# Linear attention and a four-expert block in one kernel: the attention of the next chunk put between the expert matmuls of this one

## The chip, the cores and the metric

One core of a Trainium2 chip. The metric is the device time of one execution in microseconds (us), taken over several runs; the profile is one execution, whose span is some 2 to 3 us shorter than the time. Engines: TensorE (PE for matmuls, PEld for its weight loads), VectorE (DVE), ScalarE (ACT), GpSimd (POOL); SP issues the transfers of the sync queue.

## The reference, cut to what matters

```python
# attention: B, H, S, D = 4, 8, 768, 48; f = sigmoid(f_logit)
for t in range(S):
    state = f[:, :, t, :, None] * state + einsum('bhd,bhe->bhde', k[:, :, t], v[:, :, t])
    y[:, :, t] = einsum('bhd,bhde->bhe', q[:, :, t], state)
x = y.transpose(0, 2, 1, 3).reshape(B * S, H * D)          # 3072 x 384
# four experts, F = 1024, every row goes through all of them
p = domain_probs / (domain_probs.sum(-1, keepdims=True) + 1e-09)
for e in range(4):
    out += p[:, e:e+1] * (maximum(x @ w1[e], 0) @ w2[e])
```

Both kernels cut time into 6 chunks of 128 steps. Within a chunk the attention is a masked score matmul plus a matmul with the state carried from the chunk before, so chunks of one batch follow each other. The four batches are independent.

## The kernel before

Attention first, one batch and one chunk at a time, x written to DRAM; then the experts over groups of 512 rows. The order inside each engine is chosen by a scheduler.

```python
for b in range(B):
    for c in range(C):
        # four loads of 128 x 384 f32 (q, k, v, f): runs of 192 bytes
        nc.scalar.activation(out=sig, in_=fg, func=AF.Sigmoid)
        nc.scalar.activation(out=gneg, in_=sig, func=AF.Ln)
        nc.tensor.matmul(out=cs, lhsT=Ub, rhs=gneg, ...)          # cumulative sum, 384 columns
        nc.scalar.activation(out=ecsQ, in_=cs, func=AF.Exp)
        nc.vector.reciprocal(out=ecsK, in_=ecsQ)
        # Qp = qg * ecsQ, Kp = kg * ecsK, vgb = vg, all on POOL
        # gs: 8 column sums; egs = exp(gs)
        # 16 transposes of 128 x 48 into tp, two copies to Qt, Kt
        for h in range(H):                                        # scores
            nc.tensor.matmul(out=AT_ps[:, ...], lhsT=Kt[:, ...], rhs=Qt[:, ...], ...)
        # AT = AT_ps * mask
        for h in range(H):                                        # y: 48 rows, then 128 rows
            nc.tensor.matmul(out=y_ps[:, hs], lhsT=Qt[:, ts], rhs=state_bf[:, hs], ...)
            nc.tensor.matmul(out=y_ps[:, hs], lhsT=AT[:, ts], rhs=vgb[:, hs], ...)
        # store y; KV; state = (state + KV) * egs, 8 multiplies of 48 x 48 on POOL
# ...
nc.gpsimd.dma_start(out=w1_sb, ...)       # cast f32 -> bf16, 3 MB each; no wait, so it starts early
nc.gpsimd.dma_start(out=w2_sb, ...)
for g in range(6):
    # load x, 12 transposes, then per expert e:
    for fc in range(8):
        for kk in range(3): nc.tensor.matmul(out=h_ps, ...)        # 512 columns
        nc.vector.tensor_relu(out=h_sb[:, fc, :], in_=h_ps)
    for nt in range(4):
        for fc in range(8): nc.tensor.matmul(out=o2_ps, ...)       # 384 columns
        # o_sb += p * o2_ps on DVE
```

## Time and profile before

| | us |
|---|---|
| time, median of 3 runs | 565.63 |
| span of the profiled run | 562.4 |
| attention, from the first matmul on | about 289 |
| experts | about 264 |

How the busy shares, the slices, the chain of waits and the two stretches are read is told in the prediction, with the lines.

### The profile page before, as it was taken

To read this page: it belongs to the slowest core of one execution; us is meant where nothing else is said; L and a number is where in the kernel's file an instruction comes from. 1 tells how busy PE (TensorE), PEld (TensorE's weight loads), DVE (VectorE), ACT (ScalarE), POOL (GpSimd) and SP (SyncE) were. 2 spreads that over 40 slices of the span, in tenths; PEclk is the share of its full clock that TensorE was granted. 3 is DMA by queue.
4 is the path that set the end of the run, shared out by engine and by line. 5 is a ranking of instruction groups with operands and counts; after the bars stand their busy time and mean duration, and the time that the engine had idled before them with its cause. 6 is when DMAs were issued, how large, how long until landed. Compare 5 with 4: busy or idle time off the path is not lost.

```text
span 562.4 us, 7147 instructions
## 1 busy us (share of the span) xinstructions
PE 421.2 (75%) x2760; PEld 253.2 (45%) x2784; DVE 319.7 (57%) x420; ACT 164.4 (29%) x285; POOL 139.3 (25%) x290
## 2 busy tenths in 40 slices
PE   0044158566556556566879999999999999999996
PEld 0033036445445445445654555545555555544443
DVE  1056244554554454464436776777777777677674
ACT  5096374574664674551111000000000000000000
POOL 4142364535536535635720000000000000000000
PEclk9999999999999999999999999999999999999999
DMA  9989834444443343231001101001001001001001
GB/s 165 197 143 187 158 68 94 107 92 85 103 94 80 76 94 64 63 77 41 24 23 28 30 0 58 23 7 58 1 29 58 0 1 57 2 1 56 1 0 57
DMA packets 118498, 35.12 MB, mean 62 GB/s; under 512 B 103616, under 2 KB 116928, under 8 KB 118464
## 3 DMA queue, kind: packets, MB, share of 16 engines
q1 hardware_dynamic: 112800, 28.37, 23.8%
q0 software_dynamic: 5664, 6.29, 6.7%
q8 instruction: 22, 0.36, 0.3%
q14 instruction: 12, 0.10, 0.1%
HBM read 33.87 MB, written 7.08 MB: 73 GB/s over the span
## 4 chain that ended last, share of the span: by engine, by line
PE 57%; POOL 11%; DVE 10%; issue 9%; DMA 4%; ACT 2%; SPq 0%; POOLq 0%; ACTq 0%; DVEq 0%
PE o_ps L199 23%; PE h_ps L193 22%; POOL state L145 8%; PE y_ps L130 4%; DVE ecsK L91 4%; DVE AT L120 3%; PE y_ps L128 3%; PE tp L112 3%; POOL Kp L98 3%; DVE Kt L113 2%; DMA fg<-in_f_logit_dram 2%; DMA kg<-in_k_dram 2%; PE xT_ps L182 1%; POOL Qp L97 1%; DVE h_sb L195 1%
## 5 line engine op out<-in xcount | busy, mean ns | idle before, releaser
L195 DVE TENSOR_SCALAR h_sb<-h_ps 128x512 bf16<-128x512 f32 x192 | 129.3, 692 | 26.5 <-PE h_ps L193 22.7
L199 PE MATMUL o_ps<-w_sb,h_sb 128*128 128x384 bf16 x768 | 142.9, 326 | 0.0
L193 PE MATMUL h_ps<-xT,w_sb 128*128 128x512 bf16 x552 | 139.0, 380 | 2.1 <-issue 0.2
L199 PEld LDWEIGHTS <-h_sb 128*128 128x128 bf16 x768 | 71.5, 98 | 65.2 <-DVE h_sb L195 13.6
L91 DVE RECIPROCAL ecsK<-ecsQ 128x384 f32<-128x384 f32 x24 | 61.2, 2552 | 65.7 <-POOL Kp L98 46.2
L193 PEld LDWEIGHTS <-w_sb 128*128 128x128 bf16 x576 | 56.4, 98 | 59.4 <-issue 3.4
L145 POOL TENSOR_SCALAR state<-state,egs 48x48 f32<-48x48 f32 x192 | 72.4, 398 | 3.4 <-DVE state L142 2.4
L185 ACT COPY xT<-xT_ps 128x128 bf16<-128x128 bf16 x72 | 14.3, 275 | 186.4 <-PE xT_ps L182 126.5
L205 DVE SCALAR_TENSOR_TENSOR o_sb<-o_ps,pt,o_sb 128x384 f32<-128x384 f32 x72 | 44.5, 618 | 38.3 <-PE o_ps L199 38.3
L130 PE MATMUL y_ps<-vgb,AT 128*128 128x48 bf16 x192 | 42.8, 223 | 29.9 <-DVE AT L120 29.9
L87 PE MATMUL cs<-gneg,Ub 128*128 128x384 bf16 x24 | 11.5, 480 | 63.8 <-ACT gneg L84 59.1
L130 PEld LDWEIGHTS <-AT 128*128 128x128 bf16 x192 | 20.2, 105 | 75.5 <-DVE AT L120 65.3
L113 DVE COPY Kt<-tp 48x1024 bf16<-48x1024 bf16 x24 | 16.4, 683 | 58.3 <-PE tp L112 58.3
L174 POOL TENSOR_TENSOR pt<-pt,psum 128x16 f32<-128x16 f32 x6 | 1.2, 214 | 190.1 <-DVE psum L173 190.1
L128 PE MATMUL y_ps<-state_bf,Qt 48*128 48x48 bf16 x192 | 42.3, 220 | 3.4 <-ACT state_bf L123 3.4
L102 PEld LDWEIGHTS <-gneg 128*48 128x48 bf16 x192 | 12.0, 131 | 58.2 <-issue 57.8
L94 POOL CAST vgb<-vg 128x384 bf16<-128x384 f32 x24 | 12.1, 504 | 103.7 <-PE y_ps L130 92.4
L117 PE MATMUL AT_ps<-Qt,Kt 48*128 48x128 bf16 x192 | 24.8, 308 | 8.2 <-DVE Kt L113 8.1
L123 ACT CAST state_bf<-state 48x384 bf16<-48x384 f32 x24 | 12.3, 511 | 63.7 <-POOL state L145 54.5
L120 DVE TENSOR_TENSOR AT<-AT_ps,mask 128x1024 bf16<-128x1024 f32 x24 | 28.2, 1174 | 3.3 <-PE AT_ps L117 3.3
L97 POOL TENSOR_TENSOR Qp<-qg,ecsQ 128x384 bf16<-128x384 f32 x24 | 23.7, 990 | 24.8 <-ACT egs L105 22.6
L84 ACT ACT_TABLE_LOAD x23 | 29.5, 1283 | 1.1 <-PE gs L102 0.8
(43 smaller groups left out, 368.8 us busy)
## 6 DMA issues: line engine op xcount, KB each, us to landing
w_sb<-in_moe_w_dram POOLq DMA_DIRECT2D x2, 3072.0 KB, 24.0
qg<-in_q_dram SPq DMA_DIRECT2D x24, 192.0 KB, 3.1
kg<-in_k_dram SPq DMA_DIRECT2D x24, 192.0 KB, 2.8
vg<-in_v_dram SPq DMA_DIRECT2D x24, 192.0 KB, 2.7
fg<-in_f_logit_dram SPq DMA_DIRECT2D x24, 192.0 KB, 3.3
out_dram<-o_sb SPq DMA_DIRECT2D x6, 768.0 KB, 3.6
x_bridge<-y_sb SPq DMA_DIRECT2D x24, 96.0 KB, 2.5
xt<-x_bridge SPq DMA_DIRECT2D x6, 384.0 KB, 3.4
```

What stands on the lines that cost most here:

```text
L84: nc.scalar.activation(out=gneg, in_=sig, func=AF.Ln)
L91: nc.vector.reciprocal(out=ecsK, in_=ecsQ)
L97: nc.gpsimd.tensor_tensor(out=Qp, in0=qg, in1=ecsQ, op=ALU.mult)
L113: nc.vector.tensor_copy(out=dst, in_=tp)
L120: nc.vector.tensor_tensor(out=AT, in0=AT_ps, in1=mask01, op=ALU.mult)
L128: nc.tensor.matmul(out=y_ps[:, hs], lhsT=Qt[:, ts], rhs=state_bf[:, hs], start=True, stop=False)
L130: nc.tensor.matmul(out=y_ps[:, hs], lhsT=AT[:, ts], rhs=vgb[:, hs], start=False, stop=True)
L145: nc.gpsimd.tensor_single_scalar(out=state[:, hs], in_=state[:, hs], scalar=egs[:, h:h+1], op=ALU.mult)
L193: nc.tensor.matmul(out=h_ps, lhsT=w1_sb[:, e, kk, fc*128:(fc+1)*128], rhs=xT[:, kk, :], start=(kk == 0), stop=(kk == KD - 1))
L195: nc.vector.tensor_relu(out=h_sb[:, fc, :], in_=h_ps)
L199: nc.tensor.matmul(out=o2_ps, lhsT=h_sb[:, fc, nt*128:(nt+1)*128], rhs=w2_sb[:, e, fc, :], start=(fc == 0), stop=(fc == KF - 1))
L205: nc.vector.scalar_tensor_tensor(out=o_sb[:, nt, :], in0=o2_ps, scalar=pe, in1=o_sb[:, nt, :], op0=ALU.mult, op1=ALU.add)
```

## The change

Its intent: let TensorE work on experts while the attention of the next chunk goes through its chain of engines. Chunks are now the outer loop and the four batches the inner one, so that one chunk of all batches gives 512 rows of x for the experts. x stays in SBUF; sigmoid and reciprocal are rewritten with exp and ln, so that one activation table serves; heads are processed in pairs, at partitions 0 and 64; the order of each engine is fixed by the program.

```diff
+    ctx.enter_context(tc.manual_schedule())
...
+    load(0, 0, "fqkv")
+    load(0, 1, "fqkv")
+    # pt (probabilities)
...
-            nc.scalar.activation(out=sig, in_=fg, func=AF.Sigmoid)
-            nc.scalar.activation(out=gneg, in_=sig, func=AF.Ln)
+        nc.scalar.activation(out=ex, in_=t["f"][:, hs, :], func=AF.Exp, scale=-1.0)
+        nc.scalar.activation(out=g[:, hs, 0:D], in_=ex, func=AF.Ln, bias=1.0)
...
-            nc.vector.reciprocal(out=ecsK, in_=ecsQ)
+        nc.scalar.activation(out=eK, in_=cs[:, 0:HD], func=AF.Exp)
...
+            for i in range(NP):           # 8 transposes of 128 x 112 for 16 of 128 x 48
+                nc.tensor.transpose(out=tp[:, j, i, :], in_=src[:, b, 2*i:2*i+2, :]...[:, 0:MP], ...)
...
+        for i in range(NP):               # scores: row halves in turns, on two banks
+            for r in range(2):
+                ps = slice(r * P2, r * P2 + D)
+                nc.tensor.matmul(out=A[:, r, i, :], lhsT=QK[ps, 1, i, :], rhs=QK[ps, 0, i, :], ...)
...
+            if c > 0:                     # y: one state matmul per pair, block-diagonal state
+                nc.tensor.matmul(out=y[:, i*2*D:(i+1)*2*D], lhsT=QK[:, 0, i, :], rhs=Sb[c % 2][:, b, i, :], ...)
...
+    for s in sorted(plan):                # prologue: attention of chunk 0
+        ...
+        if s >= 5 and nw:
+            load_w(*nw.pop(0))            # eight weight loads in POOL's order
...
+    load(1, 0, "fqkv")
+    load(1, 1, "fqkv")
+    for c in range(C):
+        plan = attention_plan(c + 1) if c + 1 < C else {}
+        for u in range(E * KF):           # 32 units
+            if u == 0 and c + 2 < C: load(c + 2, ...)
+            if u in (0, 2) and c + 1 < C:
+                gate(c + 1, u // 2)       # exp and ln of one half of f, on ACT
+            hp = mm_h(c, e, fc)           # 3 matmuls of 512 columns
+            relu(c, e, fc, hp)            # ACT or DVE
+            if prev is not None:
+                mm_o(prev[0], prev[1], fc)   # 4 matmuls of 384 columns, the expert before
+                ev_o(prev[0], prev[1], fc)
+            # then the attention pieces that stand at unit u
```

## The prediction

> **What bounds the kernel now.** I read the page's busy shares and slices first, then the chain that ended last, then a table of stretches, and only then the timeline.
>
> ```profile
> PE 421.2 (75%) x2760; PEld 253.2 (45%) x2784; DVE 319.7 (57%) x420; ACT 164.4 (29%) x285; POOL 139.3 (25%) x290
> ...
> PE   0044158566556556566879999999999999999996
> ...
> DMA  9989834444443343231001101001001001001001
> ...
> PE 57%; POOL 11%; DVE 10%; issue 9%; DMA 4%; ACT 2%; SPq 0%; POOLq 0%; ACTq 0%; DVEq 0%
> ```
>
> TensorE is 75% busy on average, but the slices show two programs in a row: some 21 slices at about half (attention), then 19 full ones (experts). The DMA row is full for the first five slices. The table of stretches splits the span:
>
> ```profile
> 9.00:298.00 289.00, 164.09 (x1388) 122.21 (x1389) 130.74 (x125) 149.71 (x225) 133.08 (x271) 1.00 0.50 95
> 298.00:562.40 264.40, 257.12 (x1373) 130.85 (x1394) 189.01 (x296) 11.46 (x57) 0.87 (x4) 1.00 0.07 23
> ```
>
> Columns: stretch, length, busy time of PE, PEld, DVE, ACT, POOL, then clock. In the 289 us of attention no engine is busy more than 57%: it is bound by latency from engine to engine. The 264 us of experts are TensorE's. The chain of waits there shows its rhythm:
>
> ```profile
> 300.12 1.29 PE h_ps L193 x6
> 301.42 0.33 PE o_ps L199 x2
> 301.75 1.29 PE h_ps L193 x6
> 303.04 4.70 PE o_ps L199 x28
> ```
>
> Six 512-column matmuls take 1.29 us, so 0.216 us each; two of 384 columns take 0.325, so 0.1625 each. Nothing is left to gain inside that. In the attention the repeating piece is 10.6 us per chunk of one batch (two groups of column sums (gs) in the timeline start at 152.44 and 163.06), 24 times, after a start of some 66 us in which the chain names loads:
>
> ```profile
> 37.98 11.05 DMA fg<-in_f_logit_dram
> 51.33 10.29 DMA kg<-in_k_dram
> ```
>
> These two ended late because the cast load of the expert weights was running on the other queue. The DMA view of three stretches (2 to 6, 12 to 20, 44 to 52 us) shows it:
>
> ```profile
> q1 hardware_dynamic: 4273, 0.81, 122.0%
> ...
> q0 software_dynamic: 726, 1.49, 97.6%
> q1 hardware_dynamic: 676, 0.13, 14.8%
> ...
> q0 software_dynamic: 1635, 1.26, 100.2%
> q1 hardware_dynamic: 1238, 0.23, 27.1%
> ```
>
> Columns: packets, MB, share. Alone, the loads of q, k, v and f move 4273 packets in 4 us, 1068 per us. Beside w1 (packets of 2 KB) they fall to 676 in 8 us, 84 per us; beside w2 (768 B) to 155. This line decides my number.
>
> **What the Trainium skill says.** (1) "DMA: Bandwidth & Descriptors", Queues, rings and completion order: each DMA engine takes turns between the queues it has work for, a whole packet at a time. The trace agrees: 726 packets against 676, a fair split by count, and a split of 12 to 1 by bytes. (2) "TensorE: Matmul & The Clock Gate", Back-to-back issue gap: a warm gap of N/2.4 + 2.5 ns, so 216 and 162.5 ns; the trace has both exactly. (3) The same page, LDWEIGHTS: the load takes its columns over 1.2 GHz, whatever the rows. The trace agrees for narrow loads: eight KV matmuls with 48-column weights take (0.52 - 0.217) / 7 = 0.043 us apiece. (4) "ScalarE: Activation LUTs", Table sets: the hidden batching unit: one set holds both ln and exp. It states about 2.7 us for a load on the chip; this trace has 1.283, and I use that.
>
> **The change part by part.**
> Removed: 69 activation table loads x 1.283 = 88.5 us of ACT, the reciprocals (61.2 us of DVE, now a second exp on ACT, about 0.49 us each from the ecsQ row), the x bridge through DRAM, the 192 small state multiplies on POOL (72.4 us; now four wider operations per batch and chunk). None of it is on the end's path once attention lies under the experts, so I count none of it as gain by itself. What counts is that the 289 us of attention shrink to a prologue for chunk 0, and that TensorE's own attention work is put in between the expert matmuls.
>
> Expert matmuls, unchanged: 192 x 3 x 0.216 + 192 x 4 x 0.1625 = 124.4 + 124.8 = 249.2 us.
>
> Attention on TensorE per batch and chunk, from distances in the timeline (150 to 165 us):
>
> ```profile
> 149.97 1.03 PE L117 MATMUL AT_ps<-Qt,Kt 48*128 48x128 bf16 x8 [0.46 <-DVE Kt L113]
> ...
> 150.97 1.05 PE L112 MATMUL tp<-idT,Qp 128*48 128x128 bf16 x8
> ...
> 159.60 0.52 PE L140 MATMUL KV_ps<-vgb,Kp 128*48 128x48 bf16 x8
> ```
>
> Less the latency of one (0.308, 0.312, 0.217), the first two step by 0.103 and 0.105 us. New counts: cumulative sum 0.16 + 0.10 for its weights = 0.26; 4 column sums with 112-column weights at 0.043 x 112/48 = 0.10, 0.40; 8 paired transposes (was 16) at 0.105, 0.84; 8 score matmuls at 0.103, 0.82; 12 for y (was 16 at 0.1525, now without the change between 48 and 128 rows, so 0.105), 1.26; 4 KV at 0.10, 0.40; 3 transposes of x, 0.30. Sum 4.28 us; the last chunk has no column sums and no KV: 3.48. For chunks 1 to 5: 16 x 4.28 + 4 x 3.48 = 82.4 us.
>
> Other engines per expert (10.4 + 4.2 = 14.6 us of TensorE): ACT 5 relus of about 0.6 (0.488 at 384 columns plus 128 more), 2.1 of attention, 0.8 of gates, 0.5 of copies, 6.4 us; DVE 3 x 0.692 + 3 x 0.618 + 0.68 + 1.17 + 0.7 = 6.5 us; POOL about 4.4. All hidden.
>
> Prologue. Chunk 0 is 8 loads of 2048 packets, at about 1000 per us from 2 us on: the second f lands at about 13.3, the last v at 19. ACT has both gates ahead of the first exp, so batch 0 starts at about 15. POOL takes 2.5 us a batch (0.990 + 0.990 + 0.504), and the weight loads sit in its order: two batches end at about 22, then three weight DMAs (1.1 us each to issue, from the 1.245 and 1.740 of before), and so on; batch 3 ends at about 38.5. Six more us (transpose, 0.7 copy, scores, 1.17 mask, y, copy, transpose, copy) give the first expert matmul at about 45 us.
>
> The new wait. The loads of chunk 1 stand in the sync queue behind chunk 0 and the probabilities: f and q of the first half land at about 25, just when the weights start to move. The second half of f needs 6144 packets more. The weights take 17.3 us (w1) and 21.6 us (w2), read off the stretches where they move, so until about 64; in that time the loads get 17.3 x 95 + 21.6 x 190 = 5750 packets, so that f lands at about 66 us. Its gate stands at unit 2 of the expert loop in ACT's fixed order, ahead of that unit's relu. So TensorE starts at 45, does four units of hidden matmuls, and stops at about 48 for want of a free hidden buffer. After 66 come the gate (two of 768 columns, about 0.85 each) and a relu: TensorE goes on at 68.4.
>
> Sum: 68.4, plus 249.2 + 82.4 less the 3.3 done before the stop = 396.7; plus 1 us for the first expert, which has no output matmuls to cover its relus; plus 4.5 for the last multiply (0.62), store and end (4.8 before, with a larger store) = 402.2 us of span. The times are 3.2 us above the span (565.63 against 562.4): 405.4, so I say 406 us.
>
> **The rivals.** (a) No stop at f: if the sync queue gets half by bytes, or weights move earlier, the loop runs from 45 us on: 20 us less, 383 or so. For it speaks the stretch 52 to 60 us, where the loads got 335 per us; against it the 676 packets. (b) TensorE's attention is dearer or cheaper: exposed weight loads at every change of work add perhaps 0.5 us per batch and chunk, 10 us in all (416); the two row halves of the scores running side by side, on separate banks, would take off up to 8. (c) ACT becomes the bound in the loop, a relu queuing behind exps and gates while only two hidden buffers exist: its 6.4 us of 14.6 speak against it, but a stop of 0.3 us at each of 20 batches would be 6 us. (d) POOL stalls issuing eight weight DMAs: the prologue grows, but mostly under the wait for f, so it changes little.
>
> **Range and chances.** From 388 (a mostly, or cheap attention) to 424 (b and c together). Even the worst, 68 us of start, 249 of experts and twice my attention, is 490, so slower is all but excluded: faster 0.99, same 0.005, slower 0.005.
>
> **What would show it.** Right: a TensorE gap of about 20 us soon after 45 us, ended by ACT, behind the load of f; after that TensorE over 90% busy to the end; a full expert block of some 14.6 us for chunks 0 to 4 and 10.4 for the last chunk; one table load; no store and reload of x. Wrong: a gap ended by something else, or blocks much longer than 14.6 us with ACT or DVE named before the hidden matmuls, which would mean the interleaving itself waits.

## More of the kernel before

Columns: line, engine, operation, out<-in, shapes, count; busy us, mean ns of one; idle before.

```profile
L199 PE MATMUL o_ps<-w_sb,h_sb 128*128 128x384 bf16 x768 | 142.9, 326 | 0.0
...
L87 PE MATMUL cs<-gneg,Ub 128*128 128x384 bf16 x24 | 11.5, 480 | 63.8 <-ACT gneg L84 59.1
```

The reader is to see that these two matmuls have the same shape, 128 x 128 weights and 384 columns. In the experts one takes 326 ns, in the attention 480.

## The result, and the profile after

| | before | after | predicted |
|---|---|---|---|
| time, median, us | 565.67 (4 runs) | 357.0 (4 runs) | 406 (388 to 424) |
| span of the profiled run, us | 562.4 | 354.7 | 402.2 |

The ratio of the fast runs is 0.6313, with an interval of 0.6291 to 0.6335.

The page's busy shares and slices of the changed kernel:

```profile
PE 306.0 (86%) x2218; PEld 177.2 (50%) x2256; DVE 158.7 (45%) x243; ACT 146.3 (41%) x285; POOL 104.7 (30%) x174
...
PE   0274710999999999999999999999999999999995
...
PEclk9999975799999999999999999999999999999999
DMA  8999999999901309701329201000011000010002
```

TensorE is busy in nearly all slices from the eighth on, and one hole lies before that. The DMA row is full for eleven slices (97 us). The granted clock dips at the hole. The chain of waits through the hole, in order of time (start, us, what):

```profile
23.03 37.26 DMA fg<-in_f_logit_dram
60.31 0.85 ACT ex L125
61.19 0.84 ACT gp L127
...
62.57 1.44 PE hp L278 x3
```

This is the predicted stop, link by link: the second half of f of chunk 1 is issued at 23.03 and is there 37 us later, ACT does the gate, then the relu, and TensorE goes on at 62.57 (68.4 was predicted). The DMA view of two stretches, 32 to 41 and 50 to 60 us (packets, MB, share), shows why f was late:

```profile
q0 software_dynamic: 1363, 1.46, 94.8%
q1 hardware_dynamic: 1359, 0.26, 26.3%
...
q0 software_dynamic: 1809, 1.52, 93.7%
q1 hardware_dynamic: 1807, 0.34, 31.3%
```

The two queues take turns packet by packet, to within four packets, and the weights' packets are four to six times as large. From there on the table of stretches, one for a chunk with attention and one for the last experts:

```profile
104.30:154.30 50.00, 49.29 (x379) 28.72 (x384) 25.64 (x41) 24.08 (x48) 16.26 (x28) 1.00 0.39 80
...
304.00:350.80 46.80, 46.59 (x253) 24.91 (x255) 17.95 (x28) 14.36 (x25) 0.00 (x0) 1.00 0.07 26
```

A chunk of 32 units takes 50.0 us, of which 49.3 are TensorE's. Its expert matmuls are 32 x (3 x 0.216 + 4 x 0.1625) = 41.5 us, so the attention of four batches costs 8.5 us, 2.1 us each, with the 0.7 us in which TensorE stood idle. I had predicted 4.28. That is the main error. TensorE's lines of the timeline, first from the prologue, then from the loop:

```profile
15.25 0.67 PE L167 MATMUL pt<-ident,qp 128*112 128x128 bf16 x4 [8.15 <-POOL qp L153]
...
16.67 0.53 PE L134 MATMUL pt<-gp,Ub 128*128 128x384 bf16 x1
```

```profile
212.84 0.39 PE L167 MATMUL pt<-ident,qp 128*112 128x128 bf16 x4
213.07 0.39 PE L167 MATMUL pt<-ident,kp 128*112 128x128 bf16 x4
...
214.59 0.33 PE L134 MATMUL pt<-gp,Ub 128*128 128x384 bf16 x1
```

The cumulative-sum matmul takes 0.53 us in the prologue and 0.33 in the loop, with the same operands. Four transposes start 0.23 us before the next four, a step of 0.056. The slices show a granted clock of 9 (the highest digit) in the prologue too; experiment 1 says what that digit is worth there.

### The profile page after: what moved, and what is told of

It reads as the page before. It is cut to its first block, busy times and chain, and to the rows that moved or that the text cites. A ratio compares the mean times of both kernels' runs of the same rounds, so it can differ in the third digit from the quotient of the medians.

```text
span 354.7 us, 5601 instructions
## 1 busy us (share of the span) xinstructions
PE 306.0 (86%) x2218; PEld 177.2 (50%) x2256; DVE 158.7 (45%) x243; ACT 146.3 (41%) x285; POOL 104.7 (30%) x174
## 4 chain that ended last, share of the span: by engine, by line
PE 78%; DMA 11%; SPq 6%; ACT 3%; issue 1%; DVE 0%
PE op L299 34%; PE hp L278 34%; DMA fg<-in_f_logit_dram 11%; SPq L69 6%; PE pt L167 3%; PE A L185 2%; ACT gp L127 1%; PE pt L206 1%; ACT ex L125 1%; PE pt L134 1%; PE pt L220 1%; PE pt L202 1%; PE pt L246 1%; ACT h_sb L290 1%; PE pt L137 1%
## 5 line engine op out<-in xcount | busy, mean ns | idle before, releaser
L278 PE MATMUL hp<-xT,w_sb 128*128 128x512 bf16 x538 | 154.9, 386 | 19.3 <-ACT h_sb L290 16.9
L299 PE MATMUL op<-w_sb,h_sb 128*128 128x384 bf16 x768 | 154.9, 326 | 0.3
L290 ACT ACTIVATE h_sb<-hp 128x512 bf16<-128x512 f32 x120 | 71.5, 597 | 125.7 <-PE hp L278 119.7
L288 DVE TENSOR_SCALAR h_sb<-hp 128x512 bf16<-128x512 f32 x72 | 49.7, 691 | 69.7 <-PE hp L278 68.9
L314 DVE SCALAR_TENSOR_TENSOR o_sb<-op,pn,o_sb 128x384 f32<-128x384 f32 x72 | 44.4, 617 | 63.2 <-PE op L299 55.5
L153 POOL TENSOR_TENSOR qp<-qg,eQ 128x384 bf16<-128x384 f32 x24 | 24.0, 998 | 124.3 <-ACT eQ L145 94.4
L238 POOL TENSOR_TENSOR Sf<-Sf,egs 48x192 f32<-48x192 f32 x40 | 20.1, 502 | 48.6 <-DVE Sf L230 47.0
L191 DVE TENSOR_TENSOR AT<-A,mask 128x1024 bf16<-128x1024 f32 x24 | 29.3, 1220 | 2.6 <-PE A L185 1.7
L174 DVE COPY QK<-pt 112x1024 bf16<-112x1024 bf16 x24 | 16.5, 689 | 20.7 <-PE pt L167 20.7
L155 POOL TENSOR_TENSOR kp<-kg,eK 128x384 bf16<-128x384 f32 x24 | 23.9, 996 | 0.0
```

Source lines behind the costliest of these rows:

```text
L153: nc.gpsimd.tensor_tensor(out=Qpad[c % NB][:, b, :, 0:D], in0=t["q"][:, bs, :], in1=eQ.rearrange("t (h d) -> t h d", d=D), op=ALU.mult)
L155: nc.gpsimd.tensor_tensor(out=Kpad[c % NB][:, b, :, 0:D], in0=t["k"][:, bs, :], in1=eK.rearrange("t (h d) -> t h d", d=D), op=ALU.mult)
L174: nc.vector.tensor_copy(out=QK, in_=t["tp", b])
L191: nc.vector.tensor_tensor(out=AT.rearrange("s r i t -> s (r i t)"), in0=t["A", b].rearrange("s r i t -> s (r i t)"), in1=mask01, op=ALU.mult)
L238: nc.gpsimd.tensor_tensor(out=Sf[ps, b], in0=Sf[ps, b], in1=eg, op=ALU.mult)
L278: nc.tensor.matmul(out=hp, lhsT=w1_sb[:, e, kk, fc * 128:(fc + 1) * 128], rhs=t["xT"][:, kk, :], start=(kk == 0), stop=(kk == KD - 1))
```

## The experiments

Theory A: in the attention of before, and in the prologue of after, TensorE ran at half rate because it was half idle, although the profile's granted clock reads 1.00; in the loop it has no gaps and runs at full rate, so every duration I had taken from the attention was about twice too long. Theory B: the new shapes and order (pairs of heads, row halves in turns) made the work cheaper. For the stop, theory C: the sharing with the weights starves the sync queue; its rival: only the place of f in the queue is wrong.

**1. The kernel before, kept busy.**

```diff
+    def busy(rhs, n):
+        for _ in range(n):
+            nc.tensor.matmul(out=dmy, lhsT=Ub, rhs=rhs, start=True, stop=True)
...   # after cs, after each set of transposes, after the scores and after y
+            busy(gneg, 10)
```

> The kernel before with 50 extra matmuls of 384 columns per batch and chunk, their result never read, so that TensorE has no long gaps in the attention. Theory A (in the attention of before TensorE ran at half rate because it was half idle, and the profile's granted clock does not show it): the cumulative-sum matmul falls from 479 ns towards 326 and the 48-column transpose from 314 towards 219 in most of the attention, with nothing in their shape changed. Theory B (the shapes and the order made them dear: 48 columns, one row half): they stay at 479 and 314. The total time is no test here, since the extra work costs 50 x 0.16 = 8 us a batch and chunk at full rate.

Correct. Count, then min/median/max in ns, of the cumulative sum, the transposes and the scores:

```profile
L93 PE MATMUL cs<-gneg,Ub x24: 336/336/503, 9.7 to 366.4; 128*128 128x384 bf16 x24
...
L119 PE MATMUL tp<-idT,Kp x192: 219/219/237, 40.4 to 375.4; 128*48 128x128 bf16 x192
...
L125 PE MATMUL AT_ps<-Qt,Kt x192: 216/216/227, 43.3 to 377.7; 48*128 48x128 bf16 x192
```

Before, their medians were 479, 314 and 311 ns. No shape was changed and no head paired; only the gaps were filled. Theory A's half rate holds, and B is not needed for these three durations. (The time, 654.01 us in one run, only shows the price of the extra matmuls.)

Two things have to be added. First, why the clock row hid it: the packed trace of the kernel before holds no clock record ahead of 297.66 us, that of the changed kernel none ahead of 45.17 us, and where there is no record the row reads full. The first record marks the rise: in the kernel before, expert matmuls start 0.427 us apart up to 296.71 us and 0.216 apart from 297.83 on. Second, that TensorE was slow because it was half idle is not fully separated from what it worked on. The filling was full matmuls (128 x 128 weights, 384 columns), and in the kernel before TensorE works from 156.46 to 162.63 us on narrow shapes with one pause of 0.46 us, and the transposes at the end of that stretch still start 0.107 us apart. No run filled the gaps with narrow matmuls.

**2. The changed kernel without the interleaving.**

```diff
-        plan = attention_plan(c + 1) if c + 1 < C else {}
+        plan = {}
+        nxt = attention_plan(c + 1) if c + 1 < C else {}
         for u in range(E * KF):
             ...
+        for s_ in sorted(nxt):
+            # emit the pieces, as in the prologue
```

> The changed kernel with everything but the interleaving: attention of chunk c+1 stands as one block after the experts of chunk c. Theory A: the paired transposes step and last as in the prologue (about 314 ns each instead of 219), since TensorE is half idle there, and the five blocks take 17 to 19 us each instead of 8.5 inside the experts: 357 + 5 x 9.5 = 405 us, some 5 more if each expert stage starts at half rate. Theory B: the transposes keep 219 ns in the blocks; the time then still rises to about 395 from the waits between engines.

441.15 us, ratio 0.779 (0.7762 to 0.7817); correct. The granted clock by slices, and TensorE in the first block:

```profile
PEclk9999659996679997569998669998559999589999
```

```profile
101.74 0.53 PE L134 MATMUL pt<-gp,Ub 128*128 128x384 bf16 x1
...
107.58 0.24 PE L202 MATMUL pt<-sb,QK 112*128 112x96 bf16 x1 [1.08 <-ACT egs L151]
...
108.21 0.59 PE L220 MATMUL pt<-vb,kp 128*112 128x96 bf16 x4
...
121.10 1.44 PE L278 MATMUL hp<-xT,w_sb 128*128 128x512 bf16 x3 [0.57 <-ACT xT L252]
```

The cumulative sum is back at 0.53 us with the pairs in place, so A again. The first experts after the block take 1.44 us for three matmuls, where 0.81 is usual, and the clock row shows the dips this time. I had said 405; the blocks take 19.9 to 23.1 us each (the first from 98.07 to 121.10), not 17 to 19, and TensorE stands idle for some 8 us of each. So the rest of the change is worth 125 us of the 209 (565.7 to 441.2), and the interleaving 84.

The first block also shows the new shapes at half rate. The twelve matmuls of y take 0.63 us there (107.58 to 108.21), 0.052 each, and all of the attention of one batch and chunk, summed term by term from start to start, some 3.5 us. In the loop y takes 0.39:

```profile
223.94 0.21 PE L202 MATMUL pt<-sb,QK 112*128 112x96 bf16 x1
...
224.33 0.39 PE L220 MATMUL pt<-vb,kp 128*112 128x96 bf16 x4
```

**3. Scores by row half.**

```diff
-        for i in range(NP):
-            for r in range(2):
+        for r in range(2):
+            for i in range(NP):
                 ps = slice(r * P2, r * P2 + D)
                 nc.tensor.matmul(out=A[:, r, i, :], ...)
```

> The changed kernel with the score matmuls ordered by row half (four on rows 0 to 47, then four on rows 64 to 111) and not in turns. Theory A: no change beyond 1 us (357). Theory B (taking turns between row halves is what brought the step from 0.103 to 0.041 us): 8 x 0.06 x 20 = 10 us more, 367.

358.08 us, ratio 0.6315 (0.629 to 0.634) against 0.6313: no change. Taking turns between the row halves brought nothing. But the two halves do run side by side, in either order: in the trace the eight start in pairs, 0.003 us apart with turns and 0.013 without, and 0.056 from pair to pair. What that is worth is seen beside experiment 1, where all eight use one row half at the same full rate and start 0.056 us apart one by one (first the changed kernel, then experiment 1):

```profile
217.62 0.40 PE L185 MATMUL A<-QK 48*128 48x128 bf16 x8
...
302.29 0.62 PE L125 MATMUL AT_ps<-Qt,Kt 48*128 48x128 bf16 x8
```

That is 0.22 us for each batch and chunk, an estimate of 4.4 us over 20. So for the scores theory B was right in part, in the halves and not in the turns.

**4. State matmuls of y by head.** With the right rows for each head, row halves 0 and 64 would write one bank without an order. So both heads use the first one's rows, and the numbers are wrong.

```diff
-            if c > 0:
-                nc.tensor.matmul(out=y[:, i*2*D:(i+1)*2*D], lhsT=QK[:, 0, i, :], rhs=Sb[c % 2][:, b, i, :], ...)
             for r in range(2):
                 h = 2 * i + r
+                if c > 0:
+                    nc.tensor.matmul(out=y[:, h*D:(h+1)*D], lhsT=QK[0:D, 0, i, :], rhs=Sb[c % 2][0:D, b, i, 0:D], ...)
```

> The changed kernel with the state matmuls of y one head at a time on 48 rows, as before (16 matmuls that alternate between 48 and 128 rows; both heads of a pair read the first one's rows, so the numbers are wrong on purpose, because two row halves may not write one bank). In the busy kernel before, this pattern stepped by 0.127 us at full rate, against 0.033 for the 12 paired ones here. If the alternation costs that in the loop: (16 x 0.127 - 0.39) x 20 = 33 us more, 390. If the half rate was all, 16 x 0.033 = 0.53, 3 us more, 360.

387.99 us, ratio 0.6871 (0.6826 to 0.6916): 31 us more.

```profile
218.83 0.19 PE L204 MATMUL pt<-sb,QK 48*128 48x48 bf16 x1
218.96 0.20 PE L207 MATMUL pt<-vb,AT 128*128 128x48 bf16 x1
```

At full rate, the alternation between 48 and 128 rows still steps by 0.127 us. In the changed kernel the twelve of y take 0.39 us together. So for y, theory B is right as well: the pairing alone is worth 31 us. (The pairing also leaves four matmuls fewer. That the change of rows is what costs fits the scores in the loop, which also go from 128 rows to 48 and back: about 0.09 us pass ahead of them and again behind them.) My prediction had already left this alternation out of y.

**5. Transposes by head.**

```diff
             for i in range(NP):
-                nc.tensor.transpose(out=tp[:, j, i, :], in_=src[:, b, 2*i:2*i+2, :]...[:, 0:MP], identity=ident)
+                for r in range(2):
+                    nc.tensor.transpose(out=tp[r*P2 : r*P2+(P2, D)[r], j, i, :],
+                                        in_=src[:, b, 2*i + r, 0:(P2, D)[r]], identity=ident)
```

> The changed kernel with 16 transposes (64 and 48 columns) in place of the 8 paired ones. At full rate each steps by 0.056 us, so 8 x 0.056 x 20 = 9 us more, 366. If they cost what the attention of before showed (0.105), 17 us more, 374. If the two halves, on different output partitions, run side by side, no change.

361.2 us, ratio 0.6384 (0.635 to 0.6419) against 0.6313: some 4 us more, where I had said 9. Eight transposes start 0.25 us before the next eight (221.47 and 221.72), where four paired ones take 0.23: those of two halves nearly share their time. The 4 us lie around them: some 0.09 us pass ahead of the first and again behind the last, so that the matmuls of the experts are held up by 0.66 us where paired transposes take 0.45. That is 0.21 x 20 = 4.3 us. The pairing is worth little, and what it saves is the change before and after.

**6. f of both halves first.**

```diff
-    load(1, 0, "fqkv")
-    load(1, 1, "fqkv")
+    load(1, 0, "f")
+    load(1, 1, "f")
+    load(1, 0, "qkv")
+    load(1, 1, "qkv")
```

> The changed kernel with both halves of f of chunk 1 loaded ahead of its q, k and v. If the stop at 45 to 62 us is only the order of f: it vanishes, 357 - 17 = 340 us. If it is the starved sync queue as a whole, as I think: f lands at about 23, but k and v of the first half take the places that v and f had (48 and 60 us), POOL stands in order behind v, the transposes of batch 1 (unit 9) wait until about 63; TensorE has done some 6 us more by then: about 351.

351.31 us, ratio 0.6204 (0.6182 to 0.6227). The chain of waits:

```profile
23.70 37.25 DMA vg<-in_v_dram
...
61.08 0.50 POOL vb L158
...
63.53 0.68 PE pt L167 x4
```

Whatever stands fifth in the queue of chunk 1's loads lands at 60 to 61 us. Now it is v, and the batch that POOL does after it: the stop of 16.9 us became two, of 4.0 us for k (at 46.3) and 3.6 us for this batch (at 59.0). The stop moved, as theory C has it.

**7. Late weights.** Three weight loads before the loop, the other five at units 7, 13 and 20 of its first pass; the sync queue as it was.

```diff
-        if s >= 5 and nw:
-            load_w(*nw.pop(0))
-    for w in nw:
-        load_w(*w)
+        if s == 5:
+            for _ in range(3):
+                load_w(*nw.pop(0))
+    later = {7: 2, 13: 2, 20: 1}
...
+            if c == 0:
+                for _ in range(later.get(u, 0)):
+                    load_w(*nw.pop(0))
```

> The changed kernel with only the first three weight loads (w1 of experts 0 and 1, w2 of expert 0) before the expert loop; the other five are issued inside it, at units 7, 13 and 20. The order of the sync queue is untouched. If the stop at 45 to 62 us is the packet-by-packet sharing with the weights: those three move some 2800 packets' time, 14 us, from about 22 to 37; then f of the second half needs 4400 packets at 1050 per us and lands at about 42; no stop, and no half-rate restart: 357 - 17 - 2 = 338 us. If the sync queue is late for a reason of its own: f still lands near 60 and the time stays at 357. Risk: w1 of expert 2 must be there by about 59 us; if it is late, up to 5 us come back.

338.59 us, ratio 0.5995 (0.5961 to 0.6029); correct. The chain of waits:

```profile
22.46 18.67 DMA fg<-in_f_logit_dram
```

The same load is there at 41 us and not at 60. Theory C holds: the stop was the weights' packets. Not all went as I had said: a stop of 1.9 us for f is left, and one of 1.7 us for weights that now come late; against that, the prologue is shorter, which I had not foreseen. POOL no longer issues weights ahead of batch 3, and the first expert matmul starts at 35.65 us (39.85 in the changed kernel). These 4.2 us and the 3.6 us of stops nearly cancel, so that 338 came out so closely is in part luck.

**8. Late weights and f first.** Both edits.

> Late weights and both halves of f first. As with late weights alone, about 338 us; f is then no longer near the edge, but k and v of the first half land about 2 us later each. Within 2 us of the run beside it either way.

335.01 us (334.84 to 335.26), ratio 0.5925 (0.5909 to 0.5941); correct, and the fastest here. This is 3.6 us below the run beside it, where I had said within 2: the stop of 1.9 us for f is gone, which I had taken for gone already. From the first clock record (41.12 us) to the end of the matmuls the granted clock has no dip, as in experiment 7, and one stop of 1.4 us is left, for weights:

```profile
60.54 0.81 PE L299 MATMUL op<-w_sb,h_sb 128*128 128x384 bf16 x4 [1.42 <-DMA w_sb<-in_moe_w_dram]
```

## Why the prediction was wrong, point by point

- *TensorE's attention, "4.28 us" per batch and chunk, 82.4 us in all.* This step failed. It measured 2.1 us. I took the steps 0.103 and 0.105 us "from distances in the timeline" of the attention, where TensorE ran at half rate, and added them to expert matmuls measured at full rate. By term, predicted and then measured in the loop from start to start: cumulative sum 0.26 and 0.16; column sums 0.40 and 0.18; transposes 0.84 and 0.45; scores 0.82 and 0.33, with 0.09 ahead of them; y 1.26 and 0.39; KV 0.40 and 0.22; transposes of x 0.30 and 0.17. Experiment 1 shows the half rate in the old shapes. The rate is about two thirds of the error: at half rate, in experiment 2, the same work takes some 3.5 us, in the loop 2.1. The rest of the 4.28 was too much at either rate. For y I took the step of transposes with 128 columns, 0.105 us, for matmuls of 48 and 96 columns, which step by 0.052 at half rate. For the scores I left out that the two row halves run side by side (experiment 3).
- From the restart at 62.57 to the last matmul at 350.8 are 288.2 us. Less the 246.6 of experts that remained, 41.6 are left for the attention and the restart; I had 81.7. That is 40 us of the 47.5 by which the span was off.
- *"So TensorE starts at 45 ... stops at about 48 ... goes on at 68.4."* The mechanism was right and the size was off: 39.85, about 45.7 and 62.57. f landed at 60.3, not 66. The packets per us beside the weights were not the cause: I had 5750 in the 39 us from 25 on, 147 per us, and the trace has 5157 from 25 to 60.3 us, 146 per us. (I used 95 beside w1 and 190 beside w2, where the lines I showed give 84 and 155, so this fit is in part luck.) The term that was off is the rate ahead of the weights: I had about 1000 packets per us, and it was 1196 from 6 to 12 us and 1222 from 20 to 23, so that f had fewer packets left to wait for. Weight DMAs took 0.8 to 0.9 us each of POOL, not 1.1. This is 5.8 us.
- *The end, "4.5" and "1 us for the first expert".* The end measured 3.9, from 350.8 to 354.7. The first expert's lack of output matmuls cost no pause over 0.3 us after the stop.
- *Rival (a), no stop at f,* was wrong for this kernel; its 383 would have been too high as well. *Rival (b), dearer or cheaper attention,* named the right term and one right reason: the row halves of the scores run side by side, for an estimated 4.4 us of its "up to 8". It did not see the others, and the half rate was not among my rivals. *(c)* did not occur: in the list of TensorE's waits from 64 us on no relu stands, and the longest single pause is 0.3 us. *(d)* was small; experiments 7 and 8 put the weight issues at some 4 us of the prologue.
- *The other engines hidden:* right. In the loop ACT is busy 24.1 of 50.0 us, DVE 25.6, POOL 16.3.

A check that was there to be made: the Trainium skill, "TensorE: Matmul & The Clock Gate", Single matmul latency, gives (398 + N)/2.4 ns at full rate and (219 + N)/1.2 at half. For N = 384 that is 326 and 502 ns: the expert row has the first to the digit, and the cumulative sum, at 480, is near the second. The same page, Part 1: The HAM clock gate, says that an idle TensorE falls back to half rate and that the recorded clock events are not to be trusted alone. On the first: in experiment 2 the records go to half at 100.85 us, where the longest pause of the 34 us before was 1.76 us. On the second, the records here agree with the durations from the first one on; what misled me was the stretch before it, where there is none and the clock row read 1.00.

## What to carry to other kernels

Before adding durations from two stages, compare one shape that occurs in both: if the same matmul takes 480 ns here and 326 there, the stages may have different clocks, and work that moves from the idle stage into the busy one gets cheaper (the step of a transpose went from 0.105 to 0.056 us). Take the step from matmuls of the same number of columns, too. Putting work into the gaps of a busy TensorE is then worth more than the waits it hides: TensorE stood idle for 41 us in the five blocks of experiment 2, and the interleaving brought 84. Where the clock row reads full, look whether a clock record stands there at all. And a load of large packets on a second queue takes nearly the whole transfer rate from one of small packets, since turns are by packet (146 packets per us beside the weights, some 1200 alone): hold it back until it is needed, rather than start it early because it can.

## What the Trainium skill lacked or had wrong

- "TensorE: Matmul & The Clock Gate", Part 4: it says that full rate does not engage for transposes and gives about 275 ns in a kernel. In the loop here the transposes take 219 ns and step by 0.056 us, at half rate 314 ns. So they run at full rate once other matmuls have brought it; whether transposes alone would bring it is not tested here.
- The same page, LDWEIGHTS: columns over 1.2 GHz would be 93 ns for 112 columns. At half rate, in experiment 2, the column sums with 112-column weights and one column each do step by 0.094 us; in the loop, at full rate, by 0.051. My agreement with this rule in the prediction was read at half rate; the page does not say that the time goes with the clock.
- "TensorEngine Tiling (Array Packing)", Key Properties, says that a change of tiling mode drains TensorE and gives no size. Alternating 48 and 128 rows here steps by 0.127 us, against 0.033 for twelve matmuls without the change. That this alternation is such a change of mode is my reading; the trace does not name the mode.
- "DMA: Bandwidth & Descriptors", Queues, rings and completion order, has the turns by packet right (1363 against 1359, where the profile's packet of a load is one run of 192 bytes, and the page's is 9 to 17 descriptors), but no number for what a queue of 192-byte packets keeps beside a large one: 151 packets per us here (1359 in 9 us), against 1222 with nothing beside it (3665 from 20 to 23 us).
- No page says which work counts as busy for the clock. In the kernel before, 6.2 us of narrow matmuls with one pause of 0.46 us (156.46 to 162.63 us) did not bring full rate; in experiment 2 the paired shapes, at work from 107.58 us on, have it from 111.09 on.
